# Quarter-array recurrence in blocks of 64 tokens, two batches per step, in a fused retention and feed-forward kernel

## The chip, the cores and the metric

The kernel runs on one core of one Trainium2 chip. The metric is the device time of one execution in microseconds (us). Executions of one kernel agree within some tenths of a percent to about 2%, so every kernel is run three to nine times, and times of two kernels are compared over the same rounds on the same chip. A run that lies over 1.5% above the fastest of its kernel is called slow; ratios use the fast runs alone. In the profile, PE is the matmul engine and PEld its weight loads, DVE is VectorE, ACT is ScalarE, POOL is GpSimd, and SP is the engine whose queue issues the DMA transfers. PEclk is the granted clock of the matmul engine, as a share of full speed.

## The reference, cut to what matters

```python
def _attn_ref(q, k, v):                      # (4 batches, 8 heads, 768 tokens, 64)
    for t in range(S):
        state = gamma * state + einsum('bhd,bhe->bhde', k[:, :, t], v[:, :, t])
        y[:, :, t] = scale * einsum('bhd,bhde->bhe', q[:, :, t], state)
    ...
def _moe_ref(x, w1, w2, w3, w_out):          # 3072 tokens of 512, inner width 1024
    a = x @ w1
    b = x @ w2
    return ((a * b) @ w3) @ w_out
```

The recurrence is calculated by chunks: scores of a chunk against itself, masked and multiplied by its values, plus the queries against the state that earlier chunks left. The decay is folded into scales of values, outputs and state. The product W3 x W_out is formed once at the start, so each block of tokens needs two products with 1024 columns and one with 512.

## The kernel before

A chunk is 128 tokens of one batch. A head has 64 columns, and the array has 128 rows, so keys and values are padded with zeros to the whole array (`kp`, `vp`), two heads per pair `p`.

```python
def scores(n, ...):                          # one chunk n, 8 matmuls of 128 columns
    for half in range(2):
        for i in range(2):
            for r in range(2):
                nc.tensor.matmul(ps[:, i, r, :], lhsT=kp[:, p, r, :], rhs=queries(n, p), ...)
        nc.vector.tensor_tensor(am[...], ps[...], keep[...], MULT)
def outputs(n, ...):                         # 12 matmuls of 128 columns
    for p in range(NP):
        nc.tensor.matmul(ps[:, p, :], lhsT=vp[:, p, 0, :], rhs=am[:, p, 0, :], ...)
        nc.tensor.matmul(ps[:, p, :], lhsT=vp[:, p, 1, :], rhs=am[:, p, 1, :], ...)
        if c > 0:
            nc.tensor.matmul(ps[:, p, :], lhsT=Tst[0][:, p, :], rhs=queries(n, p), ...)
def step(n):                                 # steady state; FFN units are pulled in between
    casts(n + 2); scores(n);  fill.pull(...)
    t_new = kv(n)                            # 4 matmuls, then DVE and POOL: the state
    dma_transposes(n + 2)
    load_chunk(n + 4)
    fill.pull(...); outputs(n); transposes(n + 1); fill.pull(...)
```

At the start it loads keys and values of the first four chunks as pairs of tokens, which makes rows of 512 bytes, and queries of four tokens, 1 KB rows. Later loads of keys and values have rows of 256 bytes (64 values of 4 bytes). All loads, output stores and DMA transposes are issued by SP, in the order of the program.

Of the kernel before, what the change touches and what calls it, by code (L numbers as in the profile page):

```python
# [18 lines left out]
def kernel(  # L19
# [13 lines left out]
    C = 128  # L33
    WST = 12
    NCH = S // C
    NSTEP = B * NCH
    NTOK = B * S
    DT0 = 6
    NP = H // 2
    DM = 512  # L40
    DFF = 1024

# [6 lines left out]
    xpool = ctx.enter_context(tc.tile_pool(name="xpool", bufs=4))  # L49
    ld = ctx.enter_context(tc.tile_pool(name="ld", bufs=6))  # L50
# [3 lines left out]
    ps_t = ctx.enter_context(tc.tile_pool(name="ps_t", bufs=1, space=PSUM))  # L54
    ps_at = ctx.enter_context(tc.tile_pool(name="ps_at", bufs=1, space=PSUM))
    ps_f = ctx.enter_context(tc.tile_pool(name="ps_f", bufs=3, space=PSUM))

    ctx.enter_context(tc.manual_schedule())

# [4 lines left out]
    chunk_in = {}  # L64
    q_in = {}
    pair_in = {}

    def load_pair(m, names="qkv"):

        b, c = divmod(2 * m, NCH)  # L70
        for nm, src in (("q", q), ("k", k), ("v", v)):
            if nm not in names:
                continue
            if nm == "q":
                t = ld.tile([128, 2 * 512], FP, tag="q64", name="q64", bufs=3)
                q_in[m] = t
            else:
                t = new_stage()
                pair_in[nm, m] = t
            dma_in(  # L80
                t[:, :].rearrange("p (h x) -> p h x", x=2 * D),
                src[b, :, c * C : (c + 2) * C, :].rearrange("h (p t) d -> p h (t d)", t=2),
            )

    def load_q4(half):

        t = ld.tile([128, 2 * 512], FP, tag="q64", name="q256", bufs=3)
        dma_in(
            t[:, :].rearrange("p (h x) -> p h x", x=4 * D),
            q[0, half * 4 : half * 4 + 4, 0 : 4 * C, :].rearrange("h (p t) d -> p h (t d)", t=4),  # L90
        )
        q_in["half", half] = t

    def load_chunk(n):
        if n >= NSTEP:
            return
        b, c = divmod(n, NCH)
        tiles = []
        if c % 2 == 0:

            t = ld.tile([128, 2 * 512], FP, tag="q64", name="q64", bufs=3)
            dma_in(
                t[:, :].rearrange("p (h x) -> p h x", x=2 * D),
                q[b, :, c * C : (c + 2) * C, :].rearrange("h (p t) d -> p h (t d)", t=2),
            )
            q_in[n // 2] = t
        for nm, src in (("k", k), ("v", v)):
            t = ld.tile([128, 512], FP, tag=nm + "32", name=nm + "32")
            dma_in(
                t[:, :].rearrange("p (h d) -> p h d", d=D),  # L110
                src[b, :, c * C : (c + 1) * C, :].rearrange("h i d -> i h d"),
            )
            tiles.append(t)
        chunk_in[n] = tiles
# [9 lines left out]
    def load_wo(i):  # L124

        t = new_stage()
        dma_in(
            t[:, :].rearrange("p (t n) -> p t n", t=2),
            moe_w_out[i * 256 : (i + 1) * 256, :].rearrange("(p t) n -> p t n", t=2),
        )  # L130
        return t

    def load_w3_columns(i):

        t = new_stage()
        dma_in(
            t[:, :].rearrange("p (f c) -> p f c", f=4),
            moe_w3[0:512, i * 256 : (i + 1) * 256].rearrange("(f p) c -> p f c", p=128),
        )
        return t  # L140
# [6 lines left out]
    load_q4(0)  # L147
    load_q4(1)
    load_pair(0, "kv")
    w1_st = [load_rows(moe_w1, d) for d in range(4)]  # L150
    load_pair(1, "k")
    w2_st = [load_rows(moe_w2, 0)]
    load_pair(1, "v")
    w2_st += [load_rows(moe_w2, d) for d in range(1, 4)]
    for n in range(4, 8):
        load_chunk(n)



    KP = [const.tile([128, NP, 2, 128], HP, name=f"kp{i}") for i in range(2)]  # L160
    VP = [const.tile([128, NP, 2, 128], HP, name=f"vp{i}") for i in range(3)]

    def zero(t):
        nc.vector.memset(t[:, :, :, :].rearrange("p a b c -> p (a b c)").bitcast(FP), 0.0)

    zero(VP[0])
# [5 lines left out]
    nc.gpsimd.iota(ip_i[:, :], pattern=[[0, H]], base=1, channel_multiplier=1)  # L172
    if_i = const.tile([128, 128], mybir.dt.int32, name="if_i")
    nc.gpsimd.iota(if_i[:, :], pattern=[[1, 2], [2, 64]], base=1, channel_multiplier=0)
    LGH = const.tile([128, H], FP, name="LGH")
    LGP = const.tile([128, NP], FP, name="LGP")
    for h in range(H):
# [4 lines left out]
    keep = const.tile([128, 128], FP, name="keep")  # L182
    nc.gpsimd.memset(keep[:, :], 1.0)
    nc.gpsimd.affine_select(
        out=keep[:, :], in_=keep[:, :], compare_op=mybir.AluOpType.is_ge, fill=0.0,
        base=0, pattern=[[1, 2], [2, 64]], channel_multiplier=-1,
    )

# [11 lines left out]

    keep2 = const.tile([128, 128], FP, name="keep2")
    nc.gpsimd.memset(keep2[:, :], 1.0)
    for t in range(2):
        r = slice(t * 64, t * 64 + 64)
        nc.gpsimd.affine_select(
            out=keep2[r, :], in_=keep2[r, :], compare_op=mybir.AluOpType.is_ge, fill=0.0,
            base=-t, pattern=[[1, 2], [2, 64]], channel_multiplier=-2,
        )

    ip2_i = const.tile([128, 2, H], mybir.dt.int32, name="ip2_i")  # L210
    for c in range(2):
        nc.gpsimd.iota(
            ip2_i[c * 64 : c * 64 + 64, :, :], pattern=[[1, 2], [0, H]], base=1, channel_multiplier=2
        )

    zero(KP[0])
    zero(KP[1])

    for i in (1, 2):
        nc.gpsimd.memset(VP[i][:, :, :, :].rearrange("p a b c -> p (a b c)").bitcast(FP), 0.0)  # L220
    nc.gpsimd.memset(GS[:, :, :], 0.0)
    for h in range(H):
        p, r = h // 2, (h % 2) * 64
        nc.gpsimd.memset(GS[r : r + 64, p, r : r + 64], gam[h] ** C)

    XT = {}


# [14 lines left out]
    def cast_wo(i):  # L243
        cast_to(WO[i][:, :, :].rearrange("p a n -> p (a n)"), wo_st[i][:, :], i % 2 == 1)

    def cast_w3(key, st):
        t = att.tile([128, 1024], HP, tag="w3h", name="w3h", bufs=4)
        cast_to(t[:, :], st[:, :], False)
        W3h[key] = t



    def bank(tag, shape, dtype, name):
        return (ps_t if tag == "psT" else ps_at).tile(shape, dtype, tag=tag, name=name)

    def w3_bank(key, i):
        src, tag = W3h.pop(key), ("psA1", "psK")[i % 2]
        return src, ps_at.tile([128, 1024], HP, tag=tag, name="psW3")
# [50 lines left out]


    q16s, k16s, qTs, ATs, kTs, qTd = {}, {}, {}, {}, {}, {}
    Tst = [None]

    def pair_casts(n, moved, names="kv", eng=None):

        m, c = divmod(n, 2)
        rows = slice(c * 64, c * 64 + 64)
        t = 1 - c if moved else c
        to = slice(t * 64, t * 64 + 64)
        eng = eng or (nc.vector if moved else nc.gpsimd)  # L320
        if n not in k16s:
            k16s[n] = att.tile([128, 512], HP, tag="k16", name="k16", bufs=3)
        if "k" in names:
            (nc.scalar.copy if eng is nc.scalar else eng.tensor_copy)(
                k16s[n][to, :].rearrange("i (h d) -> i h d", d=D),
                pair_in["k", m][rows, :].rearrange("i (h t d) -> i h t d", t=2, d=D)[:, :, t, :],
            )
        for r in range(2 if "v" in names else 0):
            eng.tensor_tensor(  # L329
                VP[n % 3][to, :, r, r * 64 : r * 64 + 64],  # L330
                pair_in["v", m][rows, :].rearrange("j (p s t e) -> j p s t e", s=2, t=2, e=64)[:, :, r, t, :],
                VS2[rows, t, :].rearrange("j (p s) -> j p s", s=2)[:, :, r].unsqueeze(2).broadcast_to((64, NP, 64)),
                MULT,
            )

    def q_cast(m):
        q16 = att.tile([128, 1024], HP, tag="q16", name="q16")
        nc.gpsimd.tensor_copy(  # L338
            q16[:, :].rearrange("i (t h d) -> i h t d", t=2, d=D),
            q_in.pop(m)[:, :].rearrange("i (h t d) -> i h t d", t=2, d=D),  # L340
        )
        q16s[m] = q16

    def q4_cast(half, on_act):
        q16 = att.tile([128, 1024], HP, tag="q16", name="q16")
        (nc.scalar.copy if on_act else nc.gpsimd.tensor_copy)(
            q16[:, :].rearrange("i (t h d) -> i h t d", t=4, d=D),
            q_in.pop(("half", half))[:, :].rearrange("i (h t d) -> i h t d", t=4, d=D),
        )
        q16s["half", half] = q16  # L350

    def q4_transposes(half, tag):

        q16 = q16s.pop(("half", half))
        ps = bank(tag, [128, 2, 4, 128], HP, "psTq")
        for p in range(2):
            for t in range(4):
                c0 = t * 256 + p * 128
                nc.tensor.transpose(ps[:, p, t, :], q16[:, c0 : c0 + 128], ident16[:, :])

        def back(n, on_dve=True):
            if n not in qTs:
                qTs[n] = att.tile([128, NP, 128], HP, tag="qT", name="qT", bufs=4)

            cast_to(
# [499 lines left out]
```

## Time and profile before

| | before |
|---|---|
| time, median of 3 | 194.66 us (194.63 to 194.74) |
| span of the profiled run, granted clock | 193.1 us, 1.0 |
| PE busy | 95% |
| first output product starts (read off the chain in order of time) | 46.82 us |
| 256 tokens in the steady part | 13.1 us |
| DMA queue, share of 16 engines over the span | 88.5% |

The prediction below shows the lines that bear on the bound. Two more views matter for what follows. The first is the span in 40 equal slices of 4.8 us, each digit the busy share of PE, the granted clock and the busy share of the 16 DMA engines, in tenths.

```profile
PE   6698999979999999999999999999999999999993
PEclk9999999999999999999999999999999999999999
DMA  6999999998999999999999989969979930111104
```

PE is full from the tenth slice on. The DMA is full or nearly so over the same stretch and rests only from the 33rd slice. The second view is one stretch of busy times (the columns are those explained in the prediction):

```profile
60.00:80.00 20.00, 20.00 (x204) 16.37 (x203) 14.08 (x27) 9.93 (x22) 10.95 (x15) 1.00 1.32 211
```

The DMA share of 1.32 counts overlapping packets, so anything near or over 1 is read here as full. PE has no idle time in that same stretch.

### The profile page before, as it was taken

What the parts mean: (1) busy time and instruction counts of PE and PEld (TensorE: products, weight loads), DVE (VectorE), ACT (ScalarE), POOL (GpSimd) and SP (SyncE); (2) the same over time, 40 slices, a digit from 0 to 9 for tenths busy, and PEclk for the clock granted to TensorE, in tenths of its full rate; (3) what the DMA queues carried; (4) which work ended last, traced back from release to release, by engine and by line L of the source; (5) the groups of instructions that cost most, each with busy time, mean ns of one, the idle gap of its engine ahead of it and who ended that gap; (6) DMA issues with size and microseconds to landing.
All of it is one profiled execution on the core that took longest, in us unless ns stands there. A gap on an engine that the chain in (4) does not pass through costs nothing.

```text
span 193.1 us, 4713 instructions
## 1 busy us (share of the span) xinstructions
PE 184.1 (95%) x1785; PEld 139.8 (72%) x1785; DVE 117.0 (61%) x220; ACT 103.3 (54%) x198; POOL 83.6 (43%) x144
## 2 busy tenths in 40 slices
PE   6698999979999999999999999999999999999993
PEld 2234557778797789777977797788777877887752
DVE  3225479699587758656665676565656665753220
ACT  6478598972454465354635463555355545533322
POOL 7600257728864737476252742863426432200000
PEclk9999999999999999999999999999999999999999
DMA  6999999998999999999999989969979930111104
GB/s 207 349 389 398 326 377 355 368 266 198 235 204 221 199 231 237 144 247 211 231 273 187 223 188 223 206 149 270 199 178 201 206 94 19 59 54 54 38 28 154
DMA packets 84007, 40.54 MB, mean 210 GB/s; under 512 B 61329, under 2 KB 78993, under 8 KB 83985
## 3 DMA queue, kind: packets, MB, share of 16 engines
q1 hardware_dynamic: 83984, 40.25, 88.5%
q8 instruction: 14, 0.23, 0.5%
q14 instruction: 9, 0.07, 0.2%
HBM read 29.36 MB, written 6.29 MB: 185 GB/s over the span
## 4 chain that ended last, share of the span: by engine, by line
PE 81%; DMA 10%; ACT 4%; DVE 2%; SPq 1%; issue 0%
PE psF L537 39%; PE psO L563 21%; DMA q<-in_q_dram 6%; PE psA L466 5%; DMA stg<-in_moe_w_out_dram 5%; PE psY L506 3%; PE psY L507 3%; PE psF L760 2%; PE psY L509 2%; PE psK L489 2%; SPq L62 1%; PE psG L537 1%; PE psO L580 1%; ACT w3o L241 1%; PE psG L760 1%; DVE vp L329 1%
## 5 line engine op out<-in xcount | busy, mean ns | idle before, releaser
L537 PE MATMUL psF<-xt,w 128*128 128x256 f16 (+1 forms) x736 | 85.0, 266 | 0.0
L537 PEld LDWEIGHTS <-w 128*128 128x128 f16 x768 | 68.2, 98 | 7.2
L553 DVE TENSOR_TENSOR ht<-pa,psF 128x256 f16<-128x256 f32 x88 | 36.6, 416 | 22.4 <-PE psF L537 13.1
L547 ACT COPY pa<-psF 128x256 f32<-128x256 f32 x84 | 31.3, 372 | 33.4 <-PE psF L537 33.0
L471 DVE TENSOR_TENSOR am<-psA,keep 128x512 f16<-128x512 f32 x48 | 30.9, 684 | 21.4 <-PE psA L466 21.3
L563 PE MATMUL psO<-w3o,ht 128*128 128x512 f16 x184 | 43.3, 379 | 0.0
L498 POOL TENSOR_TENSOR t<-s,GS 128x512 f16<-128x512 f32 x15 | 19.3, 1285 | 38.7 <-DVE s L497 38.7
L568 ACT ACTIVATE osb<-psO 128x512 f32<-128x512 f32 x23 | 13.7, 598 | 37.3 <-PE psO L563 37.3
L563 PEld LDWEIGHTS <-ht 128*128 128x128 f16 x184 | 17.8, 98 | 16.9 <-DVE ht L806 0.2
L383 POOL TENSOR_TENSOR vp<-v,VS 128x256 f16<-128x256 f32 x40 | 23.8, 617 | 6.9 <-DMA v<-in_v_dram 3.3
L514 DVE TENSOR_TENSOR xt<-psY,YS 128x512 f16<-128x512 f32 x24 | 17.8, 742 | 4.1 <-PE psY L509 3.8
L506 PE MATMUL psY<-am,vp 128*128 128x128 f16 x96 | 16.8, 219 | 0.9 <-POOL vp L329 0.7
L507 PE MATMUL psY<-am,vp 128*128 128x128 f16 x96 | 16.7, 219 | 0.6 <-DVE vp L329 0.6
L466 PEld LDWEIGHTS <-kp 128*128 128x128 f16 x192 | 12.5, 98 | 4.5 <-DVE kp L239 0.2
L338 POOL CAST q<-q 128x1024 f16<-128x1024 f32 x10 | 10.6, 1057 | 11.9 <-DMA q<-in_q_dram 11.9
L379 POOL CAST k<-k 128x512 f16<-128x512 f32 x20 | 12.3, 613 | 5.5 <-DMA v<-in_v_dram 2.4
L497 DVE TENSOR_TENSOR s<-psK,t 128x512 f32<-128x512 f32 x16 | 11.0, 688 | 2.8 <-PE psK L489 2.5
L262 DVE COPY w3t<-psW 128x1024 f16<-128x1024 f16 x8 | 5.5, 690 | 10.9 <-PE psW L270 8.5
L466 PE MATMUL psA<-qTd,kp 128*128 128x128 f16 x144 | 11.1, 219 | 0.0
L509 PE MATMUL psY<-qTd,t 128*128 128x128 f16 x60 | 10.8, 219 | 0.0
L440 ACT COPY kp<-kT 64x512 f16<-64x512 f16 x17 | 10.5, 618 | 0.4
L441 ACT COPY kp<-kT 64x512 f16<-64x512 f16 x17 | 10.5, 615 | 0.4
(87 smaller groups left out, 193.9 us busy)
## 6 DMA issues: line engine op xcount, KB each, us to landing
stg<-in_moe_w_dram SPq DMA_DIRECT2D x16, 512.0 KB, 8.5
q<-in_q_dram SPq DMA_DIRECT2D x12, 512.0 KB, 5.4
out_dram<-osb SPq DMA_DIRECT2D x23, 256.0 KB, 3.2
k<-in_k_dram SPq DMA_DIRECT2D x20, 256.0 KB, 5.3
v<-in_v_dram SPq DMA_DIRECT2D x20, 256.0 KB, 5.5
stg<-in_moe_w_out_dram SPq DMA_DIRECT2D x4, 512.0 KB, 8.2
stg<-in_k_dram SPq DMA_DIRECT2D x2, 512.0 KB, 9.9
stg<-in_v_dram SPq DMA_DIRECT2D x2, 512.0 KB, 9.7
```

What stands on the lines that cost most here:

```text
L383: nc.gpsimd.tensor_tensor(vp[:, :, r, r * 64 : r * 64 + 64], v32[:, :].rearrange("j (p s e) -> j p s e", s=2, e=64)[:, :, r, :], VS[:, :]. ...
L466: nc.tensor.matmul(ps[:, i, r, :], lhsT=kp[:, p, r, :], rhs=queries(n, p), start=True, stop=True)
L471: nc.vector.tensor_tensor(am[:, half * 2 : half * 2 + 2, :, :].rearrange("j p s i -> j (p s) i"), ps[:, :, :, :].rearrange("j p s i -> j ( ...
L498: eng.tensor_tensor(t16[:, :, :], s32[:, :, :], GS[:, :, :], MULT)
L506: nc.tensor.matmul(ps[:, p, :], lhsT=vp[:, p, 0, :], rhs=am[:, p, 0, :], start=True, stop=False)
L507: nc.tensor.matmul(ps[:, p, :], lhsT=vp[:, p, 1, :], rhs=am[:, p, 1, :], start=False, stop=(c == 0))
L509: nc.tensor.matmul(ps[:, p, :], lhsT=Tst[0][:, p, :], rhs=queries(n, p), start=False, stop=True)
L514: nc.vector.tensor_tensor(XT[n // 2][:, :, n % 2 * C : (n % 2 + 1) * C].rearrange("p a (i t) -> p a t i", t=2), ps[:, :, :].rearrange(orde ...
L537: nc.tensor.matmul(ps[:, i * w : (i + 1) * w], lhsT=W[d][:, (f + i) * 128 : (f + i + 1) * 128], rhs=XT[self.tok0 // TB][:, d, c0 : c0 + w] ...
L547: nc.scalar.copy(self.pa[f][:, :], ps[:, :])
L553: nc.vector.tensor_tensor(self.HT[:, f : f + TB // self.width, :].rearrange("p f n -> p (f n)"), self.pa.pop(f)[:, :], ps[:, :], MULT,)
L563: nc.tensor.matmul(psO[:, :], lhsT=self.HT[:, f, tb * 128 : (tb + 1) * 128], rhs=W3O[f][:, :], start=(f == 0), stop=(f == 7),)
```

## The change

The intent is to stop multiplying by zeros. A 64x64 product uses a quarter of the array, and products on different quarters may run at the same time. A step now handles 128 tokens of each of two batches, cut in blocks of 64; there are 12 steps of 256 tokens in place of 24 of 128. The padded copies disappear. The core of the diff:

```diff
+    L = 64
-    NSTEP = B * NCH
+    NSTEP = (B // 2) * NCH
-    load_q4(0)
-    load_q4(1)
-    load_pair(0, "kv")
+    load_q(0)                       # both batches, rows of two tokens
+    load_k(0)                       # both batches, rows of one token (256 bytes)
+    load_v(0)
 ...
+    def scores(m):                  # 32 matmuls of 64x64, 64 columns
+        for e in range(2):          # batch
+            for p in range(NP):     # pair of heads
+                for r in range(2):      # head of the pair: rows of the array
+                    for s in range(2):  # block of 64: columns of the array
+                        nc.tensor.matmul(
+                            ps[r][half(s), p * 2 + e, :], lhsT=kT[half(r), e, p, half(s)],
+                            rhs=queries(m, e, p, s, r), start=True, stop=True)
 ...
+    def inter(m):                   # with the state: row half and column half both tied to the head
+                for s, r in ((1, 0), (0, 1), (0, 0), (1, 1)):
+                    nc.tensor.matmul(
+                        ps[s][half(r), u, :], lhsT=t[s][half(r), u * L : (u + 1) * L],
+                        rhs=queries(m, e, p, s, r), start=False, ...)
 ...
+    def step(m):
+        inter(m - 1); outputs_back(m - 1, 0); outputs_back(m - 1, 1)
+        scores(m); ...; casts(m + 1)
+        k_dma(m + 1)                          # DMA transposes of keys, of queries every second step
+        q_casts(m // 2 + 1)  or  q_dma(m // 2 + 1)
+        load_q((m + 3) // 2); load(m + 2)
+        ffn[m - 2].o_unit(0); ffn[m - 2].o_unit(1)    # with the output stores
+        ...                                   # FFN of block m - 1, with intra(m) and kv(m) between
```

## The prediction

> **What bounds the kernel now.** I read four views: the page, the busy time by stretch, the chain of waits in order of time, and the waits by engine. The page comes first: its share of busy time by engine and the chain that ended last.
>
> ```profile
> PE 184.1 (95%) x1785; PEld 139.8 (72%) x1785; DVE 117.0 (61%) x220; ACT 103.3 (54%) x198; POOL 83.6 (43%) x144
> PE 81%; DMA 10%; ACT 4%; DVE 2%; SPq 1%; issue 0%
> ```
>
> The matmul stream (PE) is the bound, 81% of the chain. The DMA's 10% lies at the start. A busy PE is not proof of a full PE, so I ask how the busy time lies (columns after the stretch: busy time and count of matmuls, weight loads, DVE, ACT, POOL, granted clock, DMA share, GB/s):
>
> ```profile
> 0.00:46.82 46.82, 40.76 (x378) 26.27 (x379) 29.30 (x51) 33.29 (x49) 22.34 (x63) 1.00 1.01 326
> 118.80:131.90 13.10, 13.10 (x130) 10.49 (x128) 8.42 (x17) 6.62 (x15) 6.94 (x9) 1.00 0.95 200
> ```
>
> The first 46.8 us (weights arriving, W3 times W_out, four chunks) leave PE 6.1 us idle. Afterwards PE never waits, at full clock, while DVE, ACT and POOL rest a third of the time or more. So in the steady stretch the time is the sum of the matmul start-to-start times. The chain in order of time gives these (start us, us, what):
>
> ```profile
> 96.66 1.73 PE psO L563 x8
> 98.39 0.45 PE psA L466 x8
> 98.84 1.31 PE psF L537 x12
> 100.15 0.22 PE psK L489 x4
> ...
> 101.68 0.06 PE psY L506
> ```
>
> That is 0.216 us for an output matmul of 512 columns, 0.109 for an FFN matmul of 256, 0.056 for a recurrence matmul of 128. Per 256 tokens: FFN 64 x 0.109 + 16 x 0.216 = 10.44 us; recurrence 2 chunks x (8 scores + 4 state + 12 outputs) = 48 x 0.056 = 2.69 us. Sum 13.1 us, exactly the period that the stretch shows. The prize is therefore at most the recurrence: 24 chunks x about 1.34 = 32 us of 194.7, and every saved nanosecond of PE counts, every added one too.
>
> **What the Trainium skill says.** (1) "TensorEngine Tiling (Array Packing)", Tiling Modes, Key Properties: four 64x64 tiles load weights and multiply in parallel, but changing the tiling mode drains the engine. (2) The same page, Performance Considerations, Instruction Overhead: a matmul has about 60 cycles of overhead and a factor should not be taken from a dimension that is already small; at 2.4 GHz that is 25 ns. (3) The same page, Restrictions and Gotchas: column tiling excludes the fast weight load. (4) "TensorE: Matmul & The Clock Gate", Part 3, The mechanism: matmuls on different tiles start about 4 ns apart. The trace before runs only whole-array instructions (128*128 on every matmul row), so it confirms none of these. It does agree with full-array streaming: 128 columns in 0.056 us. And it shows what is in flight: the recorded mean of such a matmul is 219 ns against its 56 ns spacing.
>
> ```profile
> L466 PE MATMUL psA<-qTd,kp 128*128 128x128 f16 x144 | 11.1, 219 | 0.0
> L466 PEld LDWEIGHTS <-kp 128*128 128x128 f16 x192 | 12.5, 98 | 4.5 <-DVE kp L239 0.2 <-ACT kp L241 0.2
> ```
>
> **The change part by part, per 256 tokens.**
>
> Removed on PE: the 48 recurrence matmuls, 2.69 us. Added: 128 matmuls of 64x64 weights and 64 columns (32 scores, 32 within the block, 32 state updates, 32 with the state), each with its own weight load. Counted over the program in the instruction order: 384 + 384 + 352 + 384 = 1504, against 560 before. The multiplied work falls to a third: 128 x 64/4 = 2048 array columns against 48 x 128 = 6144, so if all four quarters streamed all the time it would take 2.69/3 = 0.90 us. What they really cost is the whole question:
> - Quarters overlap well: about 8 ns per matmul, 1.0 us.
> - Weight loads bind: they lose the fast load. The matmul page gives columns/1.2 ns for a load (section LDWEIGHTS), 53 ns for 64 columns: over four quarters 13.3 ns per matmul, over the two quarters that the matmuls with the state use (their rows and columns are tied to the same head) 27 ns. 96 x 13.3 + 32 x 27 = 2.1 us.
> - Issue binds at about 26 ns (the 60 cycles): 128 x 26 = 3.3 us.
>
> To this come four changes of mode per step (into and out of state+scores, into and out of block+update). A drain would expose at most 219 - 56 = 163 ns; I take 0.12 us, 0.5 us per step. So the recurrence is 1.5, 2.6 or 3.8 us against 2.69: per step -1.2, -0.1, +1.1; over 12 steps -14, -1, +13 us.
>
> Removed beside PE: the padding copies of the keys on ACT (34 of 0.62 us after DMA transposes and 13 of 0.58 from PSUM); the score masks on DVE halve (48 to 24 of 0.68 us, 16 us less); 50 value casts on POOL become 22 larger ones. Added: the state update is made twice as often per batch but on two batches at once, so its DVE count rises only from 20 to 24. By the same durations, per step DVE is 8 x 0.416 + 2 x 0.742 + 4 x 0.69 = 7.6 us, ACT 8 x 0.372 + 2 x 0.60 + 1.05 = 5.2, POOL about 2 x 1.29 for the state, 2 x 1.2 for values and 1 x 1.06 for queries, 6.1. All stay under 13 us: this relief lies off the path and is worth nothing by itself.
>
> The state chain (DVE 0.69, POOL 1.29, twice in a row, 4.0 us) starts after the state matmuls; six FFN pairs of 8 x 0.109 = 0.87 us, 5.2 us, stand before the next use. Its first half alone is needed then. Hidden, with slack.
>
> At the start the kernel before used fine steps: chunks of 128 tokens, and for keys and values of the first four chunks 512-byte rows. The new one loads them in 256-byte rows, and the whole first block (scores, mask, within, update, with state, two evictions) must pass before the FFN may begin; only 8 matmuls of W3 (1.7 us) stand beside it. The DMA is full then: its share is 1.01 in the first stretch. I put this at +2 us.
>
> **The rivals.**
> 1. *The matmul count becomes the bound.* Each quarter matmul costs as much as the 60 cycles say. For it: N is only 64, and there are 2.7 times as many instructions. Against it: the 4 ns starts of the skill. Time about 206 us.
> 2. *DMA takes PE's place.* Per step the new kernel moves the same bytes in the same small packets and transposes. In the middle the queue is already near full, and some queries arrive just in time:
>
> ```profile
> q1 hardware_dynamic: 56356, 18.99, 110.4%
> POOL q L338 <- DMA q<-in_q_dram: 11.9, 5, 4.2
> ```
>
> (the first from the DMA view of 60 to 150 us, its last column the share of 16 engines; the second from the waits, total, times and longest us.) Against it: keys and values land in 5.3 and 5.5 us and are ordered some 26 us ahead, so there is slack. If PE's step fell to 12 us, DMA could hold it there; the gain would then stop near 182 to 185 us.
> 3. *The evictions or the state chain bind.* The sums above leave 40% free; I give it little. It would show as PE waiting for DVE or POOL, and cost perhaps 5 us.
> 4. *Nothing changes*: loads bind at the middle case, near 195 us.
>
> **Range and chances.** With +2 us for the start, the three cases are 183, 195 and 210. I weigh them 0.43, 0.23, 0.34: the first most, because the matmul orders and the four PSUM banks are plainly laid out so that neighbours use different quarters, and the two blocks of quarter work are grouped to switch mode only four times. Gains past 180 are cut by DMA. The middle of this is 192 us, with 80% between 180 and 208; the edges of the 2% band are 190.8 and 198.6.
>
> **What would show it right or wrong.** In the steady step of the new trace: FFN still 0.109 and 0.216 us per matmul, and the 128 quarter matmuls in 1.0 to 3.3 us by their start-to-start times. If they take about 8 ns each, the gain is real; near 26, it is a loss. At each change between a 64*64 and a 128*128 group, a gap of 0.1 to 0.16 us. PE still busy without idle time after the start; if instead PE waits for a DMA transpose or a query load, rival 2 holds. The start: the first output matmul before began at 46.8 us; I expect 48 to 50. I am wrong if PE acquires waits for DVE or POOL, if the weight loads of quarters serialise (over 50 ns per pair, time over 230), or if the start loses more than 5 us.

## The result

| | before | after |
|---|---|---|
| time, median | 194.70 us (194.63 to 195.65, 4 runs) | 211.74 us (209.52 to 212.31, 4 runs) |
| span, clock of the profiled run | 193.1 us, 1.0 | 210.5 us, 0.95 |

The changed kernel is correct and slower: the ratio is 1.0835, with a 95% interval of 1.0769 to 1.09. Ratios in this document are the mean time of one kernel's fast runs over that of the other's of the same rounds, so not quite the ratio of the medians quoted.

The page of the changed kernel, first the busy times and the chain that ended last, by engine:

```profile
PE 182.2 (87%) x2669; PEld 126.9 (60%) x2669; DVE 98.7 (47%) x188; ACT 83.2 (40%) x158; POOL 64.0 (30%) x91
PE 53%; SPq 21%; DMA 17%; DVE 4%; ACT 2%; issue 2%; POOL 0%; ACTq 0%; POOLq 0%; DVEq 0%
```

PE held 81% of the chain and now holds 53%. SPq, the issuing queue, went from 1% to 21%. The slices show where:

```profile
PE   6789854988986049999999969999899999999994
PEclk9999999599999655999999999999999999999999
DMA  6999999999069999959479999799999961020202
```

A slice is 5.3 us here. PE has three kinds of holes: in the start (the slices with 5 and 4), the large one that ends at 78 us, and two small ones near 120 and 147 us. The clock falls to half after two of them. The DMA has a hole of its own, the 0 and the 6, at 53 to 63 us: it rests just ahead of PE's large hole. Busy times by stretch:

```profile
50.00:60.00 10.00, 9.88 (x81) 6.84 (x81) 4.31 (x8) 5.11 (x11) 5.32 (x5) 1.00 0.33 81
60.00:70.00 10.00, 5.66 (x137) 4.46 (x134) 4.25 (x9) 2.06 (x2) 2.10 (x3) 1.00 1.02 228
70.00:80.00 10.00, 3.27 (x68) 2.02 (x69) 4.54 (x9) 1.04 (x1) 6.51 (x6) 0.51 1.42 210
80.00:90.00 10.00, 10.00 (x121) 6.46 (x120) 2.95 (x7) 2.95 (x7) 1.27 (x1) 0.81 1.07 220
```

The last two numbers are DMA share and GB/s: 0.33 and 81 GB/s, while PE still worked. Then PE does little for 20 us while the DMA catches up.

**The steady step.** Where PE does not wait, the chain in order of time (start us, us, what) shows one whole step:

```profile
162.43 0.38 PE psY L376 x32
162.80 0.26 PE psK L391 x32
163.06 5.35 PE psF L450 x48
168.41 0.56 PE psY L421 x28
...
169.30 3.56 PE psO L475 x16
172.86 1.75 PE psF L450 x16
174.61 0.38 PE psY L376 x32
```

In order these are the products within the block, the state update, the FFN, the products with the state (and then the scores, some 0.3 us, in the lines left out), the output products, and the FFN again. A step takes 174.61 - 162.43 = 12.18 us; the same 256 tokens took 13.1. The quarters work: 32 matmuls on four quarters in 0.26 us are 8 ns each. The single starts in the trace say more than this mean. In the state update four matmuls on four quarters start 3 to 4 ns apart, and the next four follow 32 ns after the first four; the products with the state, on two quarters, start in pairs that also follow each other after 32 ns. So in both a quarter takes its next matmul of 64 columns 32 ns after the last. The changes of mode can be read too: from the last FFN matmul to the first quarter matmul it is 0.20 us where FFN matmuls are 0.11 apart, and on the way back the gap is about 0.1 us wider as well. Four such changes are some 0.4 us of a step.

**The large hole.** The issuing queue of SP between 47 and 80 us (start us, us, what):

```profile
47.03 3.24 SPq L62 DMA_DIRECT2D v<-in_v_dram  x2
58.00 2.08 SPq L480 DMA_DIRECT2D out_dram<-osb  x2
60.18 1.14 SPq L62 DMA_DIRECT2D k<-in_k_dram  x2
...
63.41 3.33 SPq L62 DMA_DIRECT2D q<-in_q_dram  x2
66.83 2.83 SPq L62 DMA_DIRECT2D k<-in_k_dram  x2
...
72.58 3.86 SPq L331 DMA_TRANSPOSE kT<-k  x2
```

After 50.3 us SP issues nothing until the first output blocks can be stored at 58.0, because the next load stands behind those stores in the program. The loads for block 3 (blocks are counted from 0) then go out at 60.18. The DMA transpose of its keys stands behind five pairs of loads, the first of them its own keys, and is issued at 72.58; it lands 5.17 us later, and the scores of block 3 start at 77.79. In the list of waits one line adds the values:

```profile
POOL v L288 <- DMA v<-in_v_dram: 27.5, 10, 10.0
```

The cast of values waited 10 times for its load, 27.5 us in all, 10.0 us at most.

**The start.** The chain in order of time, at the first block and at its FFN:

```profile
24.03 4.93 DMA v<-in_v_dram
...
30.37 0.45 PE psA L354 x32
...
36.91 3.57 PE psF L549 x16
```

Values land at 28.96, the first scores start at 30.37 (27.86 before), the first FFN products at 36.91 (32.54 before). These 16 matmuls of 256 columns take 3.57 us where a full clock takes 1.75: PE had waited, and the clock was halved, by the trace's clock record from 36.0 to 42.8 us. Between the landing of the values and the FFN, six steps of VectorE stand in the full chain, 4.7 us together; PE waits 1.33, 0.87 and 2.07 us for them. The first output product starts at 55.62 us; before, at 46.82.

**The sum**, worked out from these views against the span before: start +8.8; idle PE between 60 and 80 us 11.1 (20 less 5.66 and 3.27); half clock between 70 and 90 about 3.5 (3.27 x 0.49 + 10 x 0.19, an estimate); idle PE between 120 and 150 us 2.6; ten later steps at -0.92, -9.2. That is +16.8 us; the spans differ by 17.4.

### The profile page after: what moved, and what is told of

It reads as the page before. It is cut to its first block, busy times and chain, and to the rows that moved or that the text cites. A ratio compares the mean times of both kernels' runs of the same rounds, so it can differ in the third digit from the quotient of the medians.

```text
span 210.5 us, 6256 instructions
## 1 busy us (share of the span) xinstructions
PE 182.2 (87%) x2669; PEld 126.9 (60%) x2669; DVE 98.7 (47%) x188; ACT 83.2 (40%) x158; POOL 64.0 (30%) x91
## 4 chain that ended last, share of the span: by engine, by line
PE 53%; SPq 21%; DMA 17%; DVE 4%; ACT 2%; issue 2%; POOL 0%; ACTq 0%; POOLq 0%; DVEq 0%
PE psF L450 25%; SPq L62 17%; PE psO L475 15%; DMA out_dram<-osb 5%; DMA stg<-in_moe_w_out_dram 4%; PE psF L549 4%; DMA q<-in_q_dram 3%; SPq L310 2%; DMA kT<-k 2%; DMA v<-in_v_dram 2%; PE psG L450 2%; PE psY L421 2%; PE psY L376 2%; PE psA L354 1%; DVE xt L430 1%
## 5 line engine op out<-in xcount | busy, mean ns | idle before, releaser
L450 PE MATMUL psF<-xt,w 128*128 128x256 f16 x672 | 77.2, 273 | 2.6 <-ACT osb L479 2.6
L450 PEld LDWEIGHTS <-w 128*128 128x128 f16 x704 | 67.8, 98 | 13.8 <-issue 3.0
L475 PE MATMUL psO<-w3o,ht 128*128 128x512 f16 (+2 forms) x200 | 46.2, 387 | 0.0
L288 POOL TENSOR_TENSOR v<-v,VS 128x512 f16<-128x512 f32 x22 | 22.7, 1043 | 27.6 <-DMA v<-in_v_dram 27.5
L479 ACT ACTIVATE osb<-psO 128x512 f32<-128x512 f32 (+2 forms) x25 | 14.5, 580 | 40.0 <-PE psO L475 35.8
L281 ACT CAST k<-k 128x1024 f16<-128x1024 f32 (+1 forms) x12 | 11.7, 974 | 19.8 <-DMA k<-in_k_dram 11.6
L361 DVE TENSOR_TENSOR am<-psA,keep 128x512 f16<-128x512 f32 x24 | 15.3, 679 | 4.5 <-PE psA L354 4.5
L421 PE MATMUL psY<-qT,t 64*64 64x64 f16 x352 | 8.7, 198 | 8.8 <-POOL t L409 7.3
L421 PEld LDWEIGHTS <-t 64*64 64x64 f16 x352 | 7.3, 113 | 11.3 <-POOL t L409 7.6
L549 PE MATMUL psF<-xt,w 128*128 128x256 f16 x64 | 11.0, 327 | 3.3 <-DVE xt L430 2.1
L549 PEld LDWEIGHTS <-w 128*128 128x128 f16 x64 | 7.1, 117 | 5.8 <-issue 2.7
L196 ACT CAST w3h<-stg 128x1024 f16<-128x1024 f32 x8 | 8.3, 1043 | 3.8 <-DMA stg<-in_moe_w_dram 3.7
```

Source lines behind the costliest of these rows:

```text
L288: eng.tensor_tensor(v16[:, e, :].rearrange("j (h d) -> j h d", d=D), v32[:, e, :].rearrange("j (h d) -> j h d", d=D), VS[:, :].unsqueeze(2 ...
L361: nc.vector.tensor_tensor(am[:, r, :, :], ps[r][:, :, :], keep[:, :].unsqueeze(1).broadcast_to((128, NP * 2, L)), MULT,)
L421: nc.tensor.matmul(ps[s][half(r), u, :], lhsT=t[s][half(r), u * L : (u + 1) * L], rhs=queries(m, e, p, s, r), start=False, stop=(e == 1 an ...
L450: nc.tensor.matmul(ps[:, :], lhsT=W[d][:, f * 128 : (f + 1) * 128], rhs=self.x(d), start=(d == 0), stop=(d == 3),)
L475: nc.tensor.matmul(psO[:, :], lhsT=self.HT[:, f, e * 128 : (e + 1) * 128], rhs=W3O[f][:, cs], start=(f == 0), stop=(f == 7),)
L479: nc.scalar.activation(osb[:, cs], psO[:, :], AF.Copy, scale=final_scale)
```

## The experiments

Seventeen kernels were run, each beside the kernel before on the same chip. Theory A, formed after the result: the quarters save about 0.9 us per 256 tokens, and the supply (row sizes, the place of loads, stores and transposes in one queue, and a first block in one piece) takes back some 26 us. Rival B: the quarter matmuls or their mode changes are themselves the cost. Rival C: the DMA has too much work in any order.

### 1. Loads ahead of the stores, and stores on another queue

```diff
+    load(3)
+    load_q(2)
+    load(4)
     f0.o_unit(0)
 ...
-    load(3)
-    load_q(2)
-    load(4)
```

> The changed kernel with one edit: the loads of block 3, of the queries of its second group and of block 4 are issued ahead of the two output stores of the first FFN block instead of behind them. Theory A (order of issue: these loads stand in one in-order issue queue behind stores that wait for the FFN, so they start at 60 us though the queue was free at 50): the stretch from 59 to 78 us in which the matmul engine hardly works shrinks from 19 to about 8 us and the time falls from 211.7 to about 200 us. Theory B (the DMA itself is full, small rows): the data land no earlier, the time stays above 208 us.

Measured: 204.68 us (202.81 to 207.12, the last a slow run), ratio 1.0464. Three moved lines are worth 7.0 us by the medians. That is less than the 11.7 us that theory A expected, but far from theory B. The DMA share between 50 and 60 us rose from 0.33 to 0.98. The hole between 60 and 70 stayed (PE busy 5.56 of 10), with the DMA now full at 1.16.

```diff
-                nc.sync.dma_start(out[r0 : r0 + 128, cs], osb[:, cs])
+                nc.scalar.dma_start(out[r0 : r0 + 128, cs], osb[:, cs])
```

> The changed kernel with one edit: all output stores are issued from ScalarE's queue, loads and DMA transposes stay on SyncE's. Theory A: the loads no longer stand behind the stores and the stores no longer behind loads and transposes, so both the 19 us hole and the two later holes near 120 and 146 us shrink: about 197 us, a little better than the run with loads first. Theory B: no change above 1%, over 208 us.

Measured: 204.87 us, ratio 1.0512; theory A had expected 197. Taking the stores out of SP's queue is worth as much as moving the loads ahead of them, which says that the queue's order was this part of the loss, not the transfer of the stores.

> Both edits together. Theory A: like the better of the two, 194 to 199 us, since either removes the same wait at 60 us. Theory B: over 206 us.

Both together: 205.59 us, 205.07 without the one slow run, ratio 1.0507 (the profiled run is the slow one, so no trace of it is read). The two mend the same thing, and nothing is added; the time of 194 to 199 us that was expected is missed.

### 2. Neighbours on the same quarter

The loops of the second of these kernels were turned so that eight matmuls in a row use one quarter. Work and data stay the same.

```diff
-        for e in range(2):
-            for p in range(NP):
-                for s in range(2):
-                    for r in range(2):
+        for s in range(2):
+            for r in range(2):
+                for e in range(2):
+                    for p in range(NP):
```

> The kernel with both edits, and the loops of the quarter matmuls turned so that eight in a row use the same quarter of the array (the same work, the same result). Theory C (quarters only pay because neighbours use different ones): each quarter matmul goes from about 8 to 27 to 55 ns, 2.4 to 6 us more per step, so 25 to 70 us over the kernel with both edits. Rival D (the issue rate sets the pace, whatever the quarter): no change beyond 2%.

Measured: 213.91 us, ratio 1.0958 against 1.0507 in the same rounds: +8.8 us by the medians of the fast runs. One step of it, in order of time:

```profile
160.53 0.73 PE psY L376 x29
...
161.36 0.61 PE psK L391 x29
161.97 5.35 PE psF L450 x48
...
174.06 0.73 PE psY L376 x29
```

The products within the block and the state update, 64 matmuls, take 1.44 us together (160.53 to 161.97) where they took 0.63; a step takes 13.53 us in place of 12.18. By the single starts, the first matmuls on a quarter come 31 to 32 ns apart. The mean over the 64 is lower, some 22 ns with a change of mode included, since from one group of matmuls to the next the first starts of the new one lie between the last of the old. The loss of 1.35 us per step, 16 us over 12 steps, shows in part in the total; that waits absorb the rest was not checked. The expectation of 25 us and more was too high, by its 27 to 55 ns per matmul. Rival B falls: the form of the change's loops is what makes quarters pay, and they pay.

### 3. Deeper loads, transposes on PE, fewer loads

Blocks from 3 on are loaded three blocks ahead, ahead of the output products:

```diff
+        if m % 2 == 0 and m // 2 + 2 < NSTEP // 2:
+            load_q(m // 2 + 2)
+        load(m + 3)
         if m > 2:
-            if m % 2 and m + 3 < NSTEP:
-                load_q((m + 3) // 2)
-            load(m + 2)
```

> The kernel with loads first (202.8 to 207.1 us), and from block 3 on the loads of keys and values issued three blocks ahead instead of two, those of the queries one step earlier, both ahead of the output products of the step (buffers: the weight staging ones). Theory A2 (the later holes near 113 and 139 us come from a lookahead of under one step: the load is issued behind the transposes of its step and its cast blocks ScalarE): these holes go, 4 us less, about 200 us; the hole at 54 to 70 us stays. Theory B (the DMA is full on average): the holes move elsewhere and the time stays at 203 or above.

Measured: 203.34 us, ratio 1.047; no gain over the first experiment in total, where 4 us were expected. The late holes vanished, the hole at 60 to 70 us (PE 5.55 of 10) stayed, and one of 2 us lies between 90 and 120.

To this, keys of blocks 3 to 5 and one more group of queries were transposed by PE and copied back by ACT or DVE:

```diff
-        if m + 1 < NSTEP and m + 1 >= K_PE:
+        if m + 1 < NSTEP and m + 1 > 5:
             k_dma(m + 1)
 ...
+        if m + 1 <= min(5, NSTEP - 1):
+            k_transposes(m + 1, "X0", False)
```

> The same, and the keys of blocks 3 to 5 and the queries of group 2 transposed on the matmul engine instead of by DMA. It removes 5 of some 19 DMA transposes just where the DMA is behind and adds 40 matmuls of 0.056 us, 2.2 us. Theory B: the hole at 54 to 70 us shrinks by 4 to 6 us, the time by 2 to 5 us against the run before, about 196 us. Theory A2 alone: 2 us slower.

Measured: 198.04 us, ratio 1.0164 (called unclear against the kernel before), 5.3 us faster than the one before in the same rounds, with more work on the engine that is supposed to bind. Busy times of the stretch that was the hole:

```profile
60.00:70.00 10.00, 8.07 (x204) 6.58 (x204) 7.87 (x17) 3.82 (x5) 7.09 (x7) 1.00 1.16 260
```

PE works 8.07 of 10 us there, and without a break later. The DMA transposes of those blocks had landed late.

The loads of values of blocks 3 to 11 were left out of the deep version, and one block's values used for all:

> The deep-lookahead kernel with the loads of the values of blocks 3 to 11 left out (a wrong result on purpose: they use block 2's values). It takes 9 x 0.5 MB, some 27 us of 16 engines' time in 256-byte packets, off the DMA and changes no work of any engine. Theory B (DMA binds): the time falls by 8 us or more, to 192 or below. Theory A2 (only order): less than 3 us.

Measured: 195.46 us, 7.9 us less than the deep version, a little under the 8 us that theory B asked for. Both runs say that the supply up to about 80 us bounds the deep version. Both also take entries out of SP's queue, though, so the time that the queue is held and the DMA's own work are not separated. So rival C holds in part: after the queue is put in order, the supply by DMA is the bound of that stretch.

### 4. What bound the kernel before

Wrong on purpose: 176 of the output matmuls (2 of 3 where a state exists, 1 of 2 elsewhere), 176 x 0.056 = 9.8 us of PE, were taken out of the kernel before.

```diff
-            nc.tensor.matmul(ps[:, p, :], lhsT=vp[:, p, 1, :], rhs=am[:, p, 1, :], start=False, stop=(c == 0))
-            if c > 0:
-                nc.tensor.matmul(ps[:, p, :], lhsT=Tst[0][:, p, :], rhs=queries(n, p), start=False, stop=True)
```

> The kernel before with 8 of its 12 output matmuls per chunk left out (a wrong result on purpose): 176 matmuls of 0.056 us less, 10 us of matmul time. Theory E (in the kernel before the matmul engine alone binds): 184 to 186 us. Theory B (its DMA stands close behind): it gains only a part, 188 to 193 us.

Measured: 186.61 us, ratio 0.9585, between the two expectations and nearer to theory E. 8.2 of the 9.8 us arrive. The prediction's bound was right for the kernel before, and the DMA leaves room for a time of 187 us where the supply is arranged as it is there.

### 5. The start

Reorderings in the first block of the version with PE transposes: the value cast of VectorE behind the eviction of the transposed keys, the second state update behind the first output evictions, transposes of queries later.

```diff
-    v_cast(0, (nc.gpsimd, nc.vector))
     w3_mm(6, lambda: k_transposes(0, "X0", True), 3)
+    v_cast(0, (nc.gpsimd, nc.vector))
```

> The run with deep lookahead and early transposes on the matmul engine (198.0 us), with four changes of order at the start: the keys' eviction ahead of the value cast on VectorE, the second state update behind the outputs of block 0, casts of queries ahead of those of values for block 2 and its transposes between the two output products of block 0, the transposes of query group 2 behind the output products of block 1. Theory A (what is left of the loss is order at the start): the idle time of the matmul engine between 20 and 70 us falls from about 10 to 5 us, the time to about 193. Theory B (the start is set by DMA arrival alone): under 1.5 us better.

Measured: 197.29 us, ratio 1.013; the gain of 0.75 us over the version that it changes is no more than the spread of that one's runs. The idle time of PE between 20 and 70 us was to fall from about 10 to 5 us; it is 9.2 after 9.75. Eight zero matmuls in two of the waits, to keep the clock:

```diff
+    busy(3, "psF")
     inter(0)
+    busy(5, "psF")
```

> The same with eight matmuls on zeros in the two waits before the first FFN block, to keep the matmul clock up. Theory F (the half clock of 30 to 45 us costs time): the first 32 FFN matmuls at 0.109 us instead of up to 0.22, 1 to 2 us less than the run without. Rival: the matmuls on zeros only delay, same or up to 1 us slower.

Measured: 198.1 us with one slow run among four, ratio 1.0126, no gain. The start is not mended by this order within the block. The second run doesn't test what the half clock costs: in the traces of both, PE has half clock for 3.4 us, from 43.8 and from 43.9 us on (granted clock 0.91 between 37 and 56 us in both), so the zeros removed nothing. In the version that both change it was the same 3.4 us, from 37.4 us on.

The row size was tried by itself, on the kernel before: its paired loads of keys and values, 2 MB, were split so that each row is 256 bytes, into the same places.

```diff
+                for u in range(2):
+                    dma_in(
+                        t[:, :].rearrange("p (h t d) -> p h t d", t=2, d=D)[:, :, u, :],
+                        src[b, :, c * C : (c + 2) * C, :].rearrange("h (p t) d -> p h t d", t=2)[:, :, u, :],
+                    )
```

> The kernel before with the four loads of keys and values of its first four chunks (2 MB) each issued as two, in rows of 256 instead of 512 bytes, as the new kernel has them; same data in the same place. Theory G (the row size costs the new kernel part of its start: 8192 packets of 256 bytes at 23 ns against 4096 of 512 at 31 ns over 16 engines, 12 against 8 us): the first output product starts 3 to 4 us later and the time rises from 194.7 to about 197 to 199. Rival (hidden): within 1 us.

Measured: 198.01 us (197.65 to 199.13), ratio 1.0176, +3.2 us. The first output product, in order of time:

```profile
48.79 3.45 PE psO L570 x16
```

It moves from 46.82 to 48.79, 2.0 us and not the 3 to 4 expected; the time is in the range of theory G. So 256-byte rows of keys and values at the start cost some 3 us in the kernel before, of which 2.0 stand at the first output product. The edit also issues eight loads in place of four, so rows and issues are not separated, and it leaves the first queries in rows of 1 KB, where the change has 512 bytes. The other part of the +8.8 us, the whole first block of two batches that must be done before the FFN, was not isolated: the chain names it, no run takes it alone.

### 6. The start of the kernel before with the quarters behind it

These kernels keep the kernel before up to a changeover. From there on a step of quarters takes 256 tokens of one batch, that is four blocks of 64 in a chain, with the same quarter matmuls:

```python
def p_step(m):
    p_inter(m - 1); p_casts(m + 1); p_scores(m)
    p_dma(m + 1); load_p(m + 3); fill.pull(...)       # FFN
    p_intra(m); chain = p_kv(m); next(chain); fill.pull(...)
    for _ in chain: pass                              # the other three links
    fill.pull(...)
```

> The kernel before, unchanged up to the end of its first batch (six chunks of 128), and from there the quarters recurrence of the change, two chunks of the same batch per step in place of two batches (the state goes through the four blocks of 64 in turn), loads three steps ahead, the output products first in each step. Theory H (the change lost by its start and its loads, the quarters themselves gain 0.93 us per 256 tokens): 9 steps x 0.93 = 8 us less than the kernel before, 185 to 189 us, with steps of 12.2 us. Rival B (the DMA stands close behind and takes the place of the matmul engine): steps of 12.6 to 13 us, 190 to 194.

A miss: 206.12 us, ratio 1.0601, changing over at block 3 of 256, counted from 0 (58 us). The trace shows a load issued late at the changeover, and three of the four links of the state chain (DVE 0.44 and POOL 0.74 us each) in a row in front of DVE's other work. Both were to be mended: loads ahead of the transposes and a block earlier (at the start one block more than in the run above), one link between groups of FFN units.

```diff
-        next(chain)
-        for _ in chain:
-            pass
+        for _ in range(4):
+            next(chain, None)
+            fill.pull(share * (1 - SPLIT) / 4, ready)
+    load_p(4)
```

> The hybrid (start and first two blocks of the kernel before, quarters from the fourth block of 256 tokens on, two chunks of one batch per step), with the two faults of its first version mended: the loads of two more blocks are issued at the start, every later load a step earlier and ahead of the transposes, and the four links of the state chain are spread between the FFN units instead of standing in a row. Theory (quarters save about 0.9 us per 256 tokens; what was lost before lies in the supply and in the chain): nine blocks times 0.9 is 8 us, less the transition and four short chain links; 186 to 192 us, first output product unchanged at 46.8, steady steps near 12.3 us, and no hole of several us at 60 to 71. Rival (the DMA is full up to 80 us whatever the order, so the hole only moves): 194 to 203 us.

A worse miss: 210.63 us, ratio 1.0824.

> The run above, with the keys of the first two quarter blocks transposed on PE (8 matmuls and one ScalarE eviction each) instead of by the DMA. If DMA transposes that land late still hold the transition, this is 2 to 4 us faster than the run above; if the load order was the whole cause, it is the same within 0.5 us or slower by the added PE work, some 1 us.

With the keys of two blocks transposed on PE: 207.23 us, ratio 1.0638, 3.4 us less than the run above, as the first branch expected. The chain of this kernel in order of time tells why:

```profile
64.40 1.07 SPq L62
...
65.57 4.36 DMA qTd<-q
...
81.26 5.95 DMA qTd<-q
87.25 0.44 PE psX L637 x32
```

The loads put ahead had pushed the transposes of the queries behind them. SP was busy issuing loads and two stores without a break from 50.5 to 65.5 us, and the transpose that the scores waited for was issued after the last. The order of loads against stores was one fault in the change; here the order of loads against transposes was the same kind of fault, made anew by me.

So keys and queries of the first three quarter blocks were transposed on PE, loads went three blocks ahead in place of four, and the constants of the quarters (3 us of POOL at 50 us) were made during the start:

```diff
+        if m > 5:
             nc.sync.dma_start_transpose(qT[...], q16s.pop(m)[:, :])
 ...
+            if i == 2:
+                p_qtrans(m + 1)
-        load_p(m + 4)
+        load_p(m + 3)
```

> The hybrid that changes over at the third block, with keys and queries of its first three quarter blocks transposed on PE, the loads three blocks ahead, and the constants of the quarters made during the start. Before, transposes of the queries stood in the issue queue behind six loads and landed 8 to 9 us late twice. If that was the loss, the holes at 60 to 70 and 80 to 87 go and the time is 193 to 198 us. If the DMA is simply full there, the keys and values themselves come late and it stays at 200 us or more.

Measured: 195.27 us (194.86 to 196.48), ratio 1.0033: 12 us less than the one above. From 66 us on PE has hardly a gap, and steps take 12.2 us. This is three edits at once, so their shares are not separated.

The run sent with it changes over only at block 6, where two whole batches are done, and keeps DMA transposes:

> The kernel before unchanged through its first twelve chunks (two batches), where its trace shows the DMA full and PE never waiting; the last two batches by quarters, blocks of 256 tokens of one batch per step, loads three blocks ahead of their use, behind the transposes, the state chain spread between FFN units. Theory (the quarters' 0.9 us per 256 tokens is real and only the crowded first half takes it back): six blocks times 0.9 is 5.4 us, less about 1 us for the change of scheme; 189 to 191.5 us, ratio 0.97 to 0.985, PE without holes, steps of 12.2 to 12.4 us in the second half. Rival (the four-link chain or the transposes landing late bind at any place): steps of 13 us or more, 194 to 200 us.

A miss: 197.50 us, ratio 1.0131. Its steps are 12.18 us where they run, but PE has holes, of 1.3 us before 88.6 and of 3.6 us from 117 on. SP's queue ahead of the larger one:

```profile
109.86 1.88 SPq L62 DMA_DIRECT2D stg<-in_k_dram  x2
111.78 4.35 SPq L62 DMA_DIRECT2D stg<-in_v_dram  x2
116.22 1.37 SPq L759 DMA_DIRECT2D out_dram<-osb  x2
```

The loads of one block hold the queue for 6.4 us; the stores stand behind them, ACT waits for the output buffer that a store frees, and PE waits for ACT. Here too the expectation's cause (the crowded first half alone) was too narrow.

Two holes were left in the version of 195.27 us. At 52 to 55 us PE idled 1.5 us: for 1.06 us it waited for query copies behind two preparations of the exponentials in DVE's queue, for 0.38 for key copies behind the exponentials in ACT's. At 62 to 65 us two transposes shared one bank just before their use; the chain loses 2.5 us to their evictions, but PE was idle for only 1.3 us of it, since output products filled the rest. The exponentials and their preparations were moved, and the transposes put ahead:

```diff
+        if n == 5:
+            p_qtrans(3, "psK", nc.vector)
+            p_ktrans(3)
         t_new = kv(n)
```

> The last hybrid (195.3 us) with its two remaining holes closed: the exponentials of the quarters taken out of ScalarE's queue at 52 to 54 us, and the first block's two PE transposes moved some 3 us ahead of their use, on two banks, one evicted by ScalarE and one by VectorE. Theory (PE binds again, so each microsecond of hole closed shows in full): the holes at 52 to 55.4 and 62 to 65 held 1.5 and 2.5 us; 191 to 192.5 us, ratio 0.98 to 0.99. Rival (the DMA holds this stretch, and the hole opens again at the next load): 194 to 196 us.

Measured: 192.71 us (192.62 to 193.20, 4 runs) against 194.89 before, ratio 0.9885, interval 0.9869 to 0.9902. That beats both kernels, by 1.1% and, across rounds, about 9%. Its busy times show what the change had hoped for:

```profile
46.82:60.00 13.18, 13.18 (x186) 10.93 (x184) 10.16 (x22) 6.60 (x13) 9.62 (x12) 1.00 1.12 242
100.00:110.00 10.00, 10.00 (x191) 7.13 (x189) 5.44 (x12) 4.13 (x9) 3.10 (x4) 1.00 1.06 209
```

PE is full in both, at full clock, with the DMA full beside it. The spans of the two profiled runs differ by 1.5 us, which is the first hole; the medians differ by 2.6. The second hole came back at its old size (1.26 us between 60 and 70 us), now because the moved exponentials stand in ACT's queue there. So what is taken from PE's idle time arrives: PE binds this version.

What is left of the quarters' saving, worked out: nine blocks at -0.92 are -8.3 us; transposes of three blocks on PE, 8 keys and 8 queries each, cost about 1.0 per block (0.55 and 0.45 in the chain), +3.0; the hole +1.3; the first output product +0.35 (47.17 against 46.82). That is -3.6 us; measured are -2.2, so 1.4 us are not accounted for.

## Why the prediction was wrong

The prediction said 192.0 us, with 180 to 208; 211.74 is outside. Point by point:

- **The bound before was right.** PE bound it; 8.2 of 9.8 us taken from PE arrived in the time.
- **The quarters' cost was right in kind and near in size.** The first case held: the recurrence part of a step was put at 1.5 us and is 12.18 - 10.44 = 1.74, against 2.69. About 8 ns per matmul were predicted and measured on four quarters, and the four changes of mode, put at 0.5 us, cost some 0.4. What the first case left out is that the products with the state have only two quarters: they come to 16 ns each, not 8 and not the 27 of the second case. Whether their weight loads set this was not tested. The step saves 0.92 us, not 1.2. (The count of matmuls before, 560, is a slip: the trace has 544. Nothing rests on it.)
- **"I put this at +2 us", the start, failed.** It was +8.8, past the 5 us that the prediction itself had named as a sign of being wrong. Each part had been named (256-byte rows, the DMA full, the whole first block before the FFN) and none was sized. Rows cost 2.0 us at the same mark in the kernel before, and 3.2 us of its time. Half of the 8.8 had come about before the first FFN product (36.91 against 32.54), half after it. Nor did the term count the clock: it was granted at 0.84 over the 18.71 us from the first FFN product to the first output product, by estimate 3.0 us. The Trainium skill ("TensorE: Matmul & The Clock Gate", Part 1, What's actually happening) has the clock at half after an idle window of about 3.4 us. The trace agrees that the clock is halved after idling, with 16 FFN matmuls in 3.57 us for 1.75, but not on the length: no single wait between 24 and 37 us was longer than 2.07 us.
- **"Keys and values land in 5.3 and 5.5 us and are ordered some 26 us ahead, so there is slack" failed, and with it the dismissal of rival 2.** That was a fact of the kernel before, carried over to a kernel whose diff moves the loads. In the changed kernel block 3 is ordered at 60.18 us, behind stores that wait for the first FFN, 17.6 us before its scores start, with a cast and a transpose in between. PE then waits for a DMA transpose, which the prediction had named as the sign of rival 2. I read the diff for instructions per engine and not for the order in SP's queue, where it stands in plain sight. I gave rival 2 a time of 182 to 185 us, still a gain, when it was a loss.
- **"PE still busy without idle time after the start" failed** in consequence: 13.7 us of idle time between 60 and 150 us and 3.5 at half clock.
- **Rivals 1, 3 and 4 did not come.** Matmul count and the evictions did not bind in the steady part; in the start VectorE's steps did, as shown above. The state chain bound nothing there; it did in my own first hybrid, with four links in place of two.
- **The range** left the start and the supply 2 us in every case, so its upper end of 208 stood for little more than the worst case of PE alone (210; rival 1 gives 206 for the same case). An honest range needed a case with supply.

What the runs leave open is how the part of the start beyond the 256-byte rows divides, the half clock included, and which of the three edits in the 195.27 us version brought how much of its 12 us.

## What to carry to other kernels

When two engines are full at once, a change that relieves one is worth what the order of the other allows: write out the new issue queue, load by load, with what each entry waits for, and compare the time from order to use before and after. In a queue that issues in order a load must stand neither behind a store that waits for late work nor ahead of a transpose that is needed sooner. Put small matmuls on different quarters in alternation, and move the steady part first, keeping the start that was tuned.

## What the Trainium skill lacked or had wrong

- "TensorEngine Tiling (Array Packing)", Performance Considerations, Instruction Overhead: some 60 cycles (25 ns at 2.4 GHz) per matmul. Neighbours on four different quarters took 8 ns each (32 in 0.26 us), so this is no cost per matmul for the engine as a whole. On one quarter the next matmul of 64 columns came after 32 ns; whether the 60 cycles hold there was not tested with fewer columns.
- "TensorE: Matmul & The Clock Gate", Part 1, "Wait — 56ns, not 53.3ns?": start to start is said never to fall below about 25 ns. On different quarters it was 3 to 4 ns within a group of four, as the 4 ns of Part 3, The mechanism, have it; what Part 3 doesn't give is the 32 ns from one group to the next.
- "TensorEngine Tiling (Array Packing)", Tiling Modes, Key Properties: a change of mode drains the engine, without a size. Here each of the four changes of a step cost about 0.1 us, read off the single starts.
- "DMA: Bandwidth & Descriptors", Issuing engines are not separate DMA queues: issuing from several engines is said to save only sequencer time, usually small. Here stores on a second queue were worth 6.9 us, because loads no longer stood behind stores that wait for late work; and where the DMA was full, two loads held SP's queue for 4.35 us.
- No page gives what smaller rows cost a whole kernel when the transfer shares the DMA with others ("DMA: Bandwidth & Descriptors", Why small descriptors are slow, has only a cost per packet): 2 MB in rows of 256 in place of 512 bytes, in twice as many loads, cost 3.2 us here.
